# Transposing q, k and x by DMA instead of on TensorE in a fused attention and SwiGLU kernel

## The chip, the cores and the metric

One core of one Trainium2 chip runs the whole kernel. The metric is the device time of one execution in microseconds; the median of the runs stands for a kernel. The engines are named as the profile names them: PE (matrix products and transposes), DVE and ACT (element-wise work), POOL and SP (here they issue DMAs). PE writes its results to PSUM, from where DVE or ACT copies them to SBUF.

## The reference

The kernel computes causal attention in a window of 64 positions for 8 batches of 8 heads, and puts the result through a feed-forward block.

```python
B, H, S, D = q.shape                        # 8, 8, 576, 64
scores = scale * np.matmul(q, k.transpose(0, 1, 3, 2))
rel = pos[:, None] - pos[None, :]
mask = (rel >= 0) & (rel < 64)
attn = softmax(np.where(mask, scores, -1e9))
attn_out = np.matmul(attn, v)
x = attn_out.transpose(0, 2, 1, 3).reshape(B * S, H * D)     # 4608 x 512
g = x @ w_gate                                               # 512 x 1536
out = (g * sigmoid(g) * (x @ w_val)) @ w_out                 # 1536 x 512
```

Inputs and the output are float32; the kernel computes in bf16 with float32 sums.

## The kernel before

**Tiling.** The 4608 tokens are cut into 36 chunks of 128 (index n) and 9 groups of 512 (index c, four chunks each). The batches are 576 long, so four of the chunks (4, 13, 22 and 31) lie across two batches and are loaded in two parts. Attention works on chunks, the feed-forward block on groups. These are the steps; each is a method that records its operations, with what they read and write, in a graph. `emit` then gives every engine its operations in the order of recording, with semaphore waits where data or a buffer's earlier use requires them. A DMA belongs to the queue of the engine that issues it, which waits in order like any other.

- `load_qk(n)` (line 269) loads q and k of a chunk by POOL's queue, with the cast to bf16, into rings `qn` and `kn` of `NQ` = 4 buffers, 128 tokens x 512. A buffer is written again only after `T` of four chunks before has read it.
- `load_v(n)` (line 319) loads v into `va`, a ring of `NV` = 8, by POOL's queue, and then copies it by two DMAs of SP's queue (lines 332 and 336) into `vb`, which holds v shifted by 64 tokens.
- `T(n)` (line 349) transposes k and q on PE, eight 128 x 128 blocks into one PSUM bank (line 360). DVE copies k's transpose into `kT` (line 365). q's transpose goes into `qz`, a ring of `NZ` = 4: for every pair of heads it holds two operands of 128 rows, each with one head's 64 rows and 64 rows of zeros, so that a product over 128 rows gives one head's scores. ACT copies the even heads (line 366) and DVE the odd ones (line 368); the zeros are written once at the start.
- `Sx(n, half)` computes the scores of four heads (line 389), ACT their exponential into `pt` (line 401), and DVE multiplies by the mask (line 407).
- `AV(n, half)` multiplies by v (lines 419 and 420); a column of ones in v gives the sum, DVE takes its reciprocal (line 426) and writes the normalised half of a chunk's x to `xb`, a ring of four (line 429).
- `X(n)` (line 432) transposes x of a chunk on PE, four blocks (line 441), and DVE copies the result into `xT` (line 448; ACT at line 450 in the first group), a ring of `NX` = 3 groups.
- `F(c, f)` computes gate and value of 128 of the 1536 columns for one group (line 466, eight products of 512 columns), ACT a tanh (line 472) and DVE two products (lines 474 and 476) into `hT`. It reads `xT` of all four chunks of its group.
- `O(c, u)` computes the output of 128 tokens (line 489, twelve products); ACT copies it to `ost` (line 494), a ring of four, and SP's queue stores it (line 496).

**Order.** `build` writes the order out by hand. The first group's attention and feed-forward run with special steps. From line 601 on, a loop over c and u does one slot per chunk: it loads chunk n + 4 with n = 4c + u + 4, does three F of group c, both halves of AV of chunk n and of Sx of chunk n + 1, one O of group c - 1, X of chunk n and T of chunk n + 2. Below, slot n is the pass of this loop with that n, so slots 8 to 11 have c = 1 and slot 35 is the last with attention. The last x of a slot with u = 3 is needed by the next slot's first F. The slots of the last group (c = 8) have no attention left.

Of the kernel before, what the change touches and what calls it, by code (L numbers as in the profile page):

```python
# [10 lines left out]
NCH = T // 128  # L11
# [137 lines left out]

class _Kernel:  # L150
    NQ = 4
    NV = 8
    NZ = 4
    NP = 4
    NX = 3
    NH = 2
# [9 lines left out]
    def alloc(self):  # L166
        nc = self.nc

        def sb(name, n, dtype=BF):
            return nc.alloc_sbuf_tensor(name, [128, n], dtype)  # L170

        def ring(name, cnt, n, dtype=BF):
            return [sb("%s%d" % (name, i), n, dtype) for i in range(cnt)]

        self.ident = sb("ident", 128)
        self.mask = sb("mask", 4 * 64)
        self.Wg = sb("Wg", NK * DFF)[:, :].rearrange("p (c f) -> p c f", c=NK)
        self.Wv = sb("Wv", NK * DFF)[:, :].rearrange("p (c f) -> p c f", c=NK)
        self.Wo = sb("Wo", NF * DM)[:, :].rearrange("p (c m) -> p c m", c=NF)
        hd = lambda t: t[:, :].rearrange("p (h d) -> p h d", h=H)  # L180
        self.qn = [hd(t) for t in ring("qn", self.NQ, DM)]
        self.kn = [hd(t) for t in ring("kn", self.NQ, DM)]
        self.va = [hd(t) for t in ring("va", self.NV, H * 80)]
        self.vb = [hd(t) for t in ring("vb", self.NV, H * 80)]
        self.kT = sb("kT", 4 * (T + 64))[:, :].rearrange("p (c t) -> p c t", c=4)
        self.qza = sb("qz", self.NZ * 4 * 2 * 128)[:, :].rearrange("p (r c e t) -> p r c e t", r=self.NZ, c=4, e=2)
        self.qz = [self.qza[:, r] for r in range(self.NZ)]
        self.fq, self.fk = [t[:, :].rearrange("p (h j d) -> p h j d", h=H, j=4) for t in ring("f", 2, H * 256, F32)]
        self.cq, self.ck = [t[:, :].rearrange("p (j h d) -> p j h d", j=4, h=H) for t in ring("c", 2, H * 256)]
        self.nmask = sb("nmask", 4 * 64)  # L190
        self.pt = [t[:, :].rearrange("p (h x) -> p h x", h=H) for t in ring("pt", self.NP, H * 192)]
        self.rc = ring("rc", 4, 4, F32)
        self.xb = ring("xb", 4, DM)
        self.xT = [t[:, :].rearrange("p (c t) -> p c t", c=NK) for t in ring("xT", self.NX, NK * 512)]
        self.sig = ring("sig", self.NS, 512)
        self.uu = ring("uu", self.NS, 512)
        self.hT = [t[:, :].rearrange("p (f t) -> p f t", f=NF) for t in ring("hT", self.NH, NF * 512)]
        self.ost = ring("ost", self.NO, DM, F32)
        self.wup = sb("wup", 1, F32)
        self.ps = [nc.alloc_psum_tensor("ps%d" % i, [128, 512], F32) for i in range(8)]  # L200
        self.rot = {"f": ([0, 1, 2, 3], 0), "o": ([4], 0), "a": ([5, 6, 7], 0)}
        self.n_s = 0
# [18 lines left out]
    def init(self):  # L221
# [6 lines left out]
        zz = self.qza  # L228
        g.op("dve", lambda e: e.memset(zz[64:128, :, :, 0, :], 0.0), writes=[("qz", i, p, 0) for i in range(self.NZ) for p in range(4)])
        g.op("dve", lambda e: e.memset(zz[0:64, :, :, 1, :], 0.0), writes=[("qz", i, p, 1) for i in range(self.NZ) for p in range(4)])  # L230
# [4 lines left out]
    def init_pt(self):  # L235
        g = self.g
        for i in range(self.NP):
            p = self.pt[i]
            g.op("dve", lambda e, p=p: e.memset(p[:, :, 64:128], 0.0), writes=[("pt", i, 0), ("pt", i, 1)])

    def init_va(self, i0):
        g = self.g
        for i in range(i0, i0 + 4):
            va = self.va[i]
            g.op("dve", lambda e, va=va: e.memset(va[:, :, 64:80], 1.0), writes=[("va", i)])

# [22 lines left out]
    def load_qk(self, n):  # L269
        i = n % self.NQ  # L270
        for dst, src, nm in ((self.qn[i], self.q, "qn"), (self.kn[i], self.k, "kn")):
            parts = list(self.segs(128 * n, 128))
            for j, (r, b, s, L) in enumerate(parts):
                d = dst[r:r + L]
                a = src[b, :, s:s + L, :].rearrange("h p d -> p h d")
                ks = [(nm, i, j)] if len(parts) > 1 else [(nm, i, 0), (nm, i, 1)]
                self.g.op("pool", lambda e, d=d, a=a: e.dma_start(d, a), writes=ks, dma=True)  # L277

    def first_loads(self):
        for half in range(2):  # L280
# [35 lines left out]
            else:  # L316
                g.op("dve", lambda e, d=d, a=a: e.tensor_copy(d, a), reads=[bk], writes=zk)

    def load_v(self, n):
        g = self.g  # L320
        i = n % self.NV
        va = self.va[i]
        parts = list(self.segs(128 * n, 128))
        for j, (r, b, s, L) in enumerate(parts):
            d = va[r:r + L, :, 0:64]
            a = self.v[b, :, s:s + L, :].rearrange("h p d -> p h d")
            ks = [("va", i, j)] if len(parts) > 1 else [("va", i, 0), ("va", i, 1)]
            g.op("pool", lambda e, d=d, a=a: e.dma_start(d, a), writes=ks, dma=True)  # L328
        vb = self.vb[i]
        lo = [("va", i, 0), ("va", i)]  # L330
        hi = [("va", i, 0 if len(parts) == 1 else 1), ("va", i)]
        g.op("sp", lambda e: e.dma_start(vb[64:128], va[0:64]), reads=lo, writes=[("vb", i, 1)], dma=True)
        if n + 1 < NCH:
            i2 = (n + 1) % self.NV
            vb2 = self.vb[i2]
            g.op("sp", lambda e: e.dma_start(vb2[0:64], va[64:128]), reads=hi, writes=[("vb", i2, 0)], dma=True)
# [12 lines left out]
    def T(self, n):  # L349
        g = self.g  # L350
        iq, iz = n % self.NQ, n % self.NZ
        qn, kn, qz = self.qn[iq], self.kn[iq], self.qz[iz]
        bank, bk = self.bank("a")
        tb = bank[:, :].bitcast(BF).rearrange("p (w c t) -> p w c t", w=2, c=4)
        ident = self.ident

        def pe(e):
            for w, src in ((0, kn), (1, qn)):
                for c in range(4):
                    r = e.transpose(tb[:, w, c, :], src[:, 2 * c:2 * c + 2, :], ident[:, :])  # L360
            return r

        g.op("pe", pe, reads=["ident"] + [(x, iq, j) for x in ("qn", "kn") for j in range(2)], writes=[bk])
        kd = self.kT[:, :, 64 + 128 * n:64 + 128 * n + 128]
        g.op("dve", lambda e: e.tensor_copy(kd, tb[:, 0]), reads=[bk], writes=[("kT", n, p) for p in range(4)] + [(bk, "k")])  # L365
        g.op("act", lambda e: e.activation(qz[0:64, :, 0, :], tb[0:64, 1], ACTF.Copy),  # L366
             reads=[bk, (bk, "k")], writes=[("qz", iz, p, 0) for p in range(4)])
        g.op("dve", lambda e: e.tensor_copy(qz[64:128, :, 1, :], tb[64:128, 1]), reads=[bk], writes=[("qz", iz, p, 1) for p in range(4)])

    def Sx(self, n, half, bias=False):  # L370
        g = self.g
# [37 lines left out]
    def AV(self, n, half):  # L409
        g = self.g  # L410
        iv, ip, ix = n % self.NV, n % self.NP, n % 4
        va, vb, pt = self.va[iv], self.vb[iv], self.pt[ip]
# [19 lines left out]
    def X(self, n, eng="dve"):  # L432
# [16 lines left out]
        else:  # L449
            g.op("act", lambda e: e.activation(xo, tb, ACTF.Copy), reads=[bk], writes=[("xT", it, u)])  # L450

    def F(self, c, f):
        g = self.g
        it, ih = c % self.NX, c % self.NH
        xT, hT = self.xT[it], self.hT[ih]
        i = self.n_s % self.NS
# [6 lines left out]
        def mm(bank, W):  # L463
            def pe(e):
# [10 lines left out]
             reads=[("sig", i), gk], writes=[("uu", i)])  # L475
        g.op("dve", lambda e: e.scalar_tensor_tensor(hT[:, f, :], uu[:, :], 0.5, V[:, :], ALU.mult, ALU.mult),  # L476
             reads=[("uu", i), vk], writes=[("hT", ih, f)])
# [28 lines left out]
    def build(self):  # L506
        W = lambda a, b: (self.load_w("g", a, b), self.load_w("v", a, b))

        def load(n):
            if n < NCH:  # L510
                self.load_qk(n)
                self.load_v(n)

        self.first_loads()
        self.init()
# [31 lines left out]
        self.X(3, "act")  # L547
        self.banks("a", [5, 6, 7])
        self.init_va(4)
        load(4)  # L550
        load(5)
        self.load_wo(0, 6)
        self.load_wo(6, 12)
# [43 lines left out]
        self.O(0, 3)  # L597
        self.X(7)
        load(10)
        load(11)  # L600
        for c in range(1, NFC):
            for u in range(4):
                n = 4 * c + u + 4
                live = n < NCH
                load(n + 4)
                self.F(c, 3 * u)
                if live:
                    self.AV(n, 0)
                    if n + 1 < NCH:
                        self.Sx(n + 1, 0)  # L610
                self.F(c, 3 * u + 1)
                if live:
                    self.AV(n, 1)
                    if n + 1 < NCH:
                        self.Sx(n + 1, 1)
                if c > 1:
                    self.O(c - 1, u)
                if live and c > 1:
                    self.X(n)
                self.F(c, 3 * u + 2)  # L620
                if live and c == 1:
                    self.X(n)
                if n + 2 < NCH:
                    self.T(n + 2)
        self.banks("o", [0, 1, 2, 3])
        for u in range(4):
# [44 lines left out]
```

## Time and profile before

| | |
|---|---|
| median of 3 runs | 376.63 us |
| the profiled execution | 376.83 us |
| its span (first to last instruction) | 375.1 us |
| granted PE clock over the span | 1.00 |
| DMA packets, bytes | 126158, 35.61 MB |

In the profile a line such as `L466 PE MATMUL ps<-xT,Wg` names the line of the kernel, the engine, the operation, what is written and what is read; behind it stand shapes, the count, busy time and the mean of one, and the idle time of the engine just before, with what ended it. The chain is the work that ended last, followed back from the end; in its listing the columns are the start, the length and what ran. A window's row gives busy time and count for PE, PE's weight loads, DVE, ACT and POOL, then the granted clock, the DMA share (packet time over 16 engines, which can pass 1 where packets overlap) and GB/s. The rows of DMA issues end with the KB of one and the median time from issue to landing.

### The profile page before, as it was taken

What the parts mean: (1) busy time and instruction counts of PE and PEld (TensorE: products, weight loads), DVE (VectorE), ACT (ScalarE), POOL (GpSimd) and SP (SyncE); (2) the same over time, 40 slices, a digit from 0 to 9 for tenths busy, and PEclk for the clock granted to TensorE, in tenths of its full rate; (3) what the DMA queues carried; (4) which work ended last, traced back from release to release, by engine and by line L of the source; (5) the groups of instructions that cost most, each with busy time, mean ns of one, the idle gap of its engine ahead of it and who ended that gap; (6) DMA issues with size and microseconds to landing.
All of it is one profiled execution on the core that took longest, in us unless ns stands there. A gap on an engine that the chain in (4) does not pass through costs nothing.

```text
span 375.1 us, 6635 instructions
## 1 busy us (share of the span) xinstructions
PE 352.3 (94%) x2624; PEld 192.0 (51%) x2624; DVE 254.6 (68%) x550; ACT 152.3 (41%) x260; POOL 107.5 (29%) x136
## 2 busy tenths in 40 slices
PE   1589999999899999999999999999999999999986
PEld 1564555555455555555555555555555555444432
DVE  6668876688867777777777777777777777655520
ACT  2553535435444444444444444444444444233311
POOL 8985525434222222322222222422220000000000
PEclk9999999999999999999999999999999999999999
DMA  9999999979957777777888787877771000010012
GB/s 236 202 201 175 204 173 205 169 47 91 84 71 85 86 86 87 82 88 87 90 87 89 78 94 86 86 83 77 78 82 37 30 29 30 28 58 28 28 38 104
DMA packets 126158, 35.61 MB, mean 95 GB/s; under 512 B 108272, under 2 KB 121520, under 8 KB 126128
## 3 DMA queue, kind: packets, MB, share of 16 engines
q0 software_dynamic: 113152, 17.83, 64.3%
q1 hardware_dynamic: 11920, 16.31, 13.5%
q10 hardware_dynamic: 1056, 1.05, 0.9%
q8 instruction: 21, 0.34, 0.4%
q14 instruction: 9, 0.07, 0.1%
HBM read 37.75 MB, written 9.44 MB: 126 GB/s over the span
## 4 chain that ended last, share of the span: by engine, by line
PE 81%; DVE 13%; ACT 3%; DMA 2%; issue 1%
PE ps L466 41%; PE ps L489 25%; PE ps L389 5%; DVE hT L476 4%; DVE uu L474 4%; PE ps L360 3%; PE ps L441 2%; PE ps L420 2%; PE ps L419 2%; DVE xb L429 2%; DMA f<-in_q_dram 2%; ACT sig L472 1%; DVE pt L407 1%; ACT qz L366 1%; PE ps L302 1%
## 5 line engine op out<-in xcount | busy, mean ns | idle before, releaser
L474 DVE SCALAR_TENSOR_TENSOR uu<-sig,ps 128x512 bf16<-128x512 bf16 x108 | 74.1, 686 | 65.1 <-ACT sig L472 65.1
L466 PE MATMUL ps<-xT,Wg 128*128 128x512 bf16 x432 | 111.0, 380 | 2.4 <-DVE xT L448 1.7
L466 PE MATMUL ps<-xT,Wv 128*128 128x512 bf16 x432 | 110.9, 379 | 0.0
L489 PE MATMUL ps<-Wo,hT 128*128 128x512 bf16 x432 | 98.7, 380 | 2.1 <-DVE hT L476 2.1
L472 ACT ACTIVATE sig<-ps 128x512 bf16<-128x512 f32 x108 | 64.0, 592 | 43.4 <-PE ps L466 43.4
L277 POOL DMA_DIRECT2D qn<-in_q_dram x36 | 30.4, 847 | 164.2 <-PE ps L360 161.3
L476 DVE SCALAR_TENSOR_TENSOR hT<-uu,ps 128x512 bf16<-128x512 bf16 x108 | 74.2, 687 | 3.7
L466 PEld LDWEIGHTS ps<-xT,Wv 128*128 128x128 bf16 x432 | 42.2, 98 | 51.0
L489 PEld LDWEIGHTS ps<-Wo,hT 128*128 128x128 bf16 x432 | 40.9, 98 | 46.9 <-DVE hT L476 2.7
L401 ACT ACTIVATE pt<-ps 128x512 bf16<-128x512 f32 x72 | 42.9, 596 | 33.2 <-PE ps L389 30.5
L466 PEld LDWEIGHTS ps<-xT,Wg 128*128 128x128 bf16 x432 | 38.2, 98 | 32.6 <-DVE xT L448 2.0
L494 ACT ACTIVATE ost<-ps 128x512 f32<-128x512 f32 x36 | 21.5, 597 | 74.8 <-PE ps L489 74.8
L366 ACT ACTIVATE qz<-ps 64x512 bf16<-64x512 bf16 x32 | 18.9, 590 | 57.8 <-DVE kT L365 57.8
L328 POOL DMA_DIRECT2D va<-in_v_dram x40 | 34.7, 875 | 1.3 <-DVE wup L226 0.8
L389 PE MATMUL ps<-qz,kT 128*128 128x128 bf16 x288 | 30.8, 225 | 2.0 <-ACT qz L366 0.4
L429 DVE TENSOR_TENSOR xb<-ps,rc 128x256 bf16<-128x256 f32 x72 | 30.6, 425 | 2.5
L277 POOL DMA_DIRECT2D kn<-in_k_dram x36 | 30.7, 858 | 1.2 <-DMA Wv<-in_moe_w_val_dram 0.8
L448 DVE COPY xT<-ps 128x512 bf16<-128x512 bf16 x32 | 13.6, 423 | 24.1 <-PE ps L441 24.1
L407 DVE TENSOR_TENSOR pt<-pt,mask 128x512 bf16<-128x512 bf16 x64 | 26.6, 416 | 1.5 <-ACT pt L401 1.4
L419 PE MATMUL ps<-vb,pt 128*128 128x65 bf16 x288 | 26.9, 194 | 0.1
L420 PE MATMUL ps<-va,pt 128*128 128x65 bf16 x288 | 27.0, 194 | 0.0
L419 PEld LDWEIGHTS ps<-vb,pt 128*128 128x128 bf16 x288 | 22.6, 98 | 7.3 <-DVE xT L448 0.2
(44 smaller groups left out, 198.6 us busy)
## 6 DMA issues: line engine op xcount, KB each, us to landing
out_dram<-ost SPq DMA_DIRECT2D x36, 256.0 KB, 2.0
vb<-va SPq DMA_DIRECT2D x71, 80.0 KB, 2.1
va<-in_v_dram POOLq DMA_DIRECT2D x32, 128.0 KB, 4.5
qn<-in_q_dram POOLq DMA_DIRECT2D x28, 128.0 KB, 3.4
kn<-in_k_dram POOLq DMA_DIRECT2D x28, 128.0 KB, 4.4
Wo<-in_moe_w_out_dram POOLq DMA_DIRECT2D x2, 768.0 KB, 19.2
Wg<-in_moe_w_gate_dram POOLq DMA_DIRECT2D x5, 256.0 KB, 12.7
Wv<-in_moe_w_val_dram POOLq DMA_DIRECT2D x5, 256.0 KB, 13.3
```

Source lines behind the costliest of these rows:

```text
L277: self.g.op("pool", lambda e, d=d, a=a: e.dma_start(d, a), writes=ks, dma=True)
L328: g.op("pool", lambda e, d=d, a=a: e.dma_start(d, a), writes=ks, dma=True)
L389: r = e.matmul(sv[:, w, c], self.kT[:, pr, k0:k0 + 128], qz[:, pr, :, 64 * w:64 * w + 64], start=not bias, stop=True)
L401: g.op("act", lambda e: e.activation(po, si, ACTF.Exp, scale=SCALE), reads=[bk], writes=[pk])
L419: e.matmul(av[:, j, :], pt[:, h, 0:128], vb[:, h, 0:65], start=True, stop=False)
L420: r = e.matmul(av[:, j, :], pt[:, h, 64:192], va[:, h, 0:65], start=False, stop=True)
L429: g.op("dve", lambda e: e.tensor_tensor(xo, av[:, :, 0:64], rb, ALU.mult), reads=[bk, ("rc", ir)], writes=[("xb", ix, half)])
L466: r = e.matmul(bank[:, :], W[:, kk, f * 128:f * 128 + 128], xT[:, kk, :], start=(kk == 0), stop=(kk == NK - 1))
L472: g.op("act", lambda e: e.activation(sig[:, :], G[:, :], ACTF.Tanh, scale=0.5), reads=[gk], writes=[("sig", i)])
L474: g.op("dve", lambda e: e.scalar_tensor_tensor(uu[:, :], sig[:, :], 1.0, G[:, :], ALU.add, ALU.mult), reads=[("sig", i), gk], writes=[("uu ...
L476: g.op("dve", lambda e: e.scalar_tensor_tensor(hT[:, f, :], uu[:, :], 0.5, V[:, :], ALU.mult, ALU.mult), reads=[("uu", i), vk], writes=[(" ...
L489: r = e.matmul(OB[:, :], hT[:, f, 128 * u:128 * u + 128], self.Wo[:, f, :], start=(f == 0), stop=(f == NF - 1))
```

## The change

- For chunks n >= `ND` = 12, which are prepared in the slots from c = 1, u = 1 on, `T(n)` is replaced by `TD(n)`: two transposing DMAs of SP's queue, one of k from `kn` to `kT` and one of q from `qd` to `qz`.
- `qd` is a new ring of four. q is loaded into it by two DMAs of POOL's queue, even heads and odd heads, each into its 64 of 128 columns; the other columns are zeroed once (`init_qd`). The transpose of this is `qz` with its zeros.
- `TD(n + 3)` is recorded after the first part of slot n, where `T(n + 2)` stood at the end of slot n.
- In the slots with c > 1, `X(n)` is replaced by `XD(n)`: one transposing DMA of SP's queue from `xb` to `xT`. It is recorded ahead of O, where X stood behind it.
- The copies of v (`copy_v`) are taken out of the load: for the chunks loaded in and just ahead of the loop they are recorded in slot n for chunk n + 3, behind XD (or behind X where c = 1).
- The ring of v shrinks from 8 to 6.

```diff
-    NV = 8
+    NV = 6
+    ND = 12
...
+        self.qd = [t[:, :].rearrange("p (c e x) -> p c e x", c=4, e=2) for t in ring("qd", 4, 1024)]
...
+    def init_qd(self):
+        for i in range(4):
+            for e_ in range(2):
+                d = self.qd[i][:, :, e_, 64 - 64 * e_:128 - 64 * e_]
+                self.g.op("dve", lambda e, d=d: e.memset(d, 0.0), writes=[("qd", i, 0), ("qd", i, 1)])
...
-        for i in range(i0, i0 + 4):
+        for i in range(i0, min(i0 + 4, self.NV)):
...
-                d = dst[r:r + L]
                 a = src[b, :, s:s + L, :].rearrange("h p d -> p h d")
-                ks = [(nm, i, j)] if len(parts) > 1 else [(nm, i, 0), (nm, i, 1)]
-                self.g.op("pool", lambda e, d=d, a=a: e.dma_start(d, a), writes=ks, dma=True)
+                ds, nk = [dst[r:r + L]], nm
+                if nm == "qn" and n >= self.ND:
+                    qd = self.qd[i][r:r + L]
+                    ds, nk = [qd[:, :, 0, 0:64], qd[:, :, 1, 64:128]], "qd"
+                ks = [(nk, i, j)] if len(parts) > 1 else [(nk, i, 0), (nk, i, 1)]
+                for z, d in enumerate(ds):
+                    az = a if len(ds) == 1 else src[b, z::2, s:s + L, :].rearrange("h p d -> p h d")
+                    kz = ks if len(ds) == 1 else [k + (z,) for k in ks]
+                    self.g.op("pool", lambda e, d=d, a=az: e.dma_start(d, a), writes=kz, dma=True)
...
+    def TD(self, n):
+        g = self.g
+        iq, iz = n % self.NQ, n % self.NZ
+        kn, qd = self.kn[iq], self.qd[iq]
+        kd = self.kT[:, :, 64 + 128 * n:192 + 128 * n]
+        ka = kn.rearrange("p h d -> p (h d)")
+        g.op("sp", lambda e: e.dma_start_transpose(kd, ka), reads=[("kn", iq, 0), ("kn", iq, 1)],
+             writes=[("kT", n, p) for p in range(4)], dma=True)
+        qo = self.qz[iz].rearrange("p c e t -> p (c e) t")
+        qa = qd.rearrange("p c e x -> p (c e x)")
+        g.op("sp", lambda e: e.dma_start_transpose(qo, qa),
+             reads=[("qd", iq, j) for j in range(2)] + [("qd", iq, j, z) for j in range(2) for z in range(2)],
+             writes=[("qz", iz, p, e) for p in range(4) for e in range(2)], dma=True)
...
+    def XD(self, n):
+        ix, it, u = n % 4, (n // 4) % self.NX, n % 4
+        xb = self.xb[ix]
+        xo = self.xT[it][:, :, 128 * u:128 * u + 128]
+        self.g.op("sp", lambda e: e.dma_start_transpose(xo, xb[:, :]), reads=[("xb", ix, 0), ("xb", ix, 1)],
+                  writes=[("xT", it, u)], dma=True)
...
         load(10)
-        load(11)
+        load(11, False)
         for c in range(1, NFC):
             for u in range(4):
                 n = 4 * c + u + 4
                 live = n < NCH
-                load(n + 4)
+                load(n + 4, False)
                 self.F(c, 3 * u)
                 if live:
                     self.AV(n, 0)
                     if n + 1 < NCH:
                         self.Sx(n + 1, 0)
+                if n + 3 < NCH and n + 3 >= self.ND:
+                    self.TD(n + 3)
                 self.F(c, 3 * u + 1)
                 if live:
                     self.AV(n, 1)
                     if n + 1 < NCH:
                         self.Sx(n + 1, 1)
+                if live and c > 1:
+                    self.XD(n)
+                    if n + 3 < NCH:
+                        self.copy_v(n + 3)
                 if c > 1:
                     self.O(c - 1, u)
-                if live and c > 1:
-                    self.X(n)
                 self.F(c, 3 * u + 2)
                 if live and c == 1:
                     self.X(n)
+                    self.copy_v(n + 3)
-                if n + 2 < NCH:
+                if n + 2 < NCH and n + 2 < self.ND:
                     self.T(n + 2)
```

More of the change, by code (lines that the diff above doesn't have):

```diff
@@ L317, in first_T, with load_v @@
                 g.op("dve", lambda e, d=d, a=a: e.tensor_copy(d, a), reads=[bk], writes=zk)
-    def load_v(self, n):
+    def load_v(self, n, copy=True):
         g = self.g
@@ L328, in load_v, with copy_v @@
             g.op("pool", lambda e, d=d, a=a: e.dma_start(d, a), writes=ks, dma=True)
+        if copy:
+            self.copy_v(n)
+    def copy_v(self, n):
+        g = self.g
+        i = n % self.NV
+        va = self.va[i]
+        parts = list(self.segs(128 * n, 128))
         vb = self.vb[i]
@@ L368, in T @@
         g.op("dve", lambda e: e.tensor_copy(qz[64:128, :, 1, :], tb[64:128, 1]), reads=[bk], writes=[("qz", iz, p, 1) for p in range(4)])
+    def TD(self, n):
+        g = self.g
+        iq, iz = n % self.NQ, n % self.NZ
[9 more added lines that the diff above has]
+             writes=[("qz", iz, p, e) for p in range(4) for e in range(2)], dma=True)
     def Sx(self, n, half, bias=False):
@@ L507, in build, with load @@
         W = lambda a, b: (self.load_w("g", a, b), self.load_w("v", a, b))
-        def load(n):
+        def load(n, copy=True):
             if n < NCH:
                 self.load_qk(n)
-                self.load_v(n)
+                self.load_v(n, copy)
         self.first_loads()
@@ L549, in build @@
         self.init_va(4)
+        self.init_qd()
         load(4)
```

## The prediction

> **What bounds the kernel now.** I read the page first: busy times, and the shares of the chain that ended last.
>
> ```profile
> span 375.1 us, 6635 instructions
> PE 352.3 (94%) x2624; PEld 192.0 (51%) x2624; DVE 254.6 (68%) x550; ACT 152.3 (41%) x260; POOL 107.5 (29%) x136
> PE 81%; DVE 13%; ACT 3%; DMA 2%; issue 1%
> ```
>
> PE is busy for 94% and carries 81% of the chain. That is an average, so I next read the chain in order of time around 200 us, in the part where attention and the feed-forward products run together (windows, then the last two lines from a later stretch of the same chain).
>
> ```profile
> 200.17 2.59 PE ps L489 x12
> 202.76 0.22 PE ps L441 x4
> 202.98 1.73 PE ps L466 x8
> 204.71 0.45 PE ps L360 x8
> 205.16 1.73 PE ps L466 x8
> 207.41 1.73 PE ps L466 x8
> 209.81 1.29 PE ps L489 x6
> ```
>
> ```profile
> 332.34 2.59 PE ps L489 x12
> 340.11 2.59 PE ps L489 x12
> ```
>
> A slot (one pass of the loop of lines 601 to 624, called by its n) is 209.81 - 200.17 = 9.64 us long, and every piece in it is PE: three F of 1.73, one O of 2.59, X of 0.22, T of 0.45, and the rest AV and Sx. Without attention, in the last group, a slot is 340.11 - 332.34 = 7.77 = 3 x 1.73 + 2.59. PE waits for nobody here, so what leaves PE in these slots comes off the time one for one, as long as nothing else becomes late.
>
> **The change, part by part.**
>
> *Transposes leave PE.* T(n) goes for n = 12 to 35 (it stood in slots 10 to 33), and X(n) goes for n = 12 to 35 (slots 12 to 35): 24 of each. By the chain's rows that is 24 x (0.45 + 0.22) = 16.1 us of PE. No PE work is added. A full slot becomes 9.64 - 0.67 = 8.97 us.
>
> *Copies out of PSUM leave DVE and ACT.*
>
> ```profile
> L366 ACT ACTIVATE qz<-ps 64x512 bf16<-64x512 bf16 x32 | 18.9, 590 | 57.8 <-DVE kT L365 57.8
> L368 DVE COPY qz<-ps 64x512 bf16<-64x512 bf16 x32 | 13.7, 427 | 1.0
> L448 DVE COPY xT<-ps 128x512 bf16<-128x512 bf16 x32 | 13.6, 423 | 24.1 <-PE ps L441 24.1
> L365 DVE COPY kT<-ps 128x512 bf16<-128x512 bf16 x32 | 13.3, 417 | 0.0
> ```
>
> Per slot 0.43 + 0.42 + 0.42 = 1.27 us of DVE and 0.59 us of ACT. DVE is 68% busy and off the path in these slots, so this is worth nothing by itself; it only lets xb be ready earlier (below).
>
> *Zeroing qd.* Eight memsets of 128 x 256 elements are added to DVE and two of the eight small ones on va go.
>
> ```profile
> 24.71 0.59 DVE L245 MEMSET va<- 128x128 bf16 x4
> 27.58 0.69 DVE L474 SCALAR_TENSOR_TENSOR uu<-sig,ps 128x512 bf16<-128x512 bf16 x1 [2.29 <-ACT sig L472]
> L225 DVE MEMSET mask<- 128x256 bf16 x1 | 0.3, 272 | 0.0
> ```
>
> At the row of the same size they cost 8 x 0.272 = 2.2 us, less 2 x 0.15 = 0.3. They stand right behind the memsets at 24.71, where DVE then waits 2.29 us for the first sig. 1.9 fits into that: price 0. If that cover were gone, it would be up to 1.9 us, once.
>
> *POOL.* Each of the 24 chunks loads q by two DMAs instead of one; three of them (13, 22, 31) lie across a batch and take two more instead of one, so 27 issues are added. v's ring goes from 8 to 6, so the load of v(n+4) now waits for AV(n-2); behind it on POOL stand q and k of n+5, which the transpose needs only in slot n+2.
>
> ```profile
> POOL qn L277 <- PE ps L360: 161.3, 27, 8.1
> SPq L496 <- ACT ost L494: 249.0, 35, 9.3
> ```
>
> ```profile
> 203.42 0.34 SPq L496 DMA_DIRECT2D out_dram<-ost  x1
> 203.80 0.46 SPq L332 DMA_DIRECT2D vb<-va  x1
> 204.30 0.60 SPq L336 DMA_DIRECT2D vb<-va  x1
> 207.34 0.90 POOL L328 DMA_DIRECT2D va<-in_v_dram  x1
> ```
>
> At 0.9 us an issue POOL goes from three to four issues, 3.6 us of a slot of 8.97. It waits 161.3 us in 27 times today, up to 8.1 us a time, so this is hidden: 0.
>
> *SP.* Three transposes (k, q, x) join one output and two copies of v. At the rows above, 0.34 to 0.60 us an issue, they add 1.0 to 1.8 us a slot; SP's queue waits up to 9.3 us for ost. I take 1.5 and price it at 0. The order within a slot is: k and q of n+3, then x of n, then the copies of v, then the output. The wait that is added is x's, for xb. Behind it are the copies, for vb that is read three slots later, and the output, whose buffers form a ring of four. Nobody waits for either.
>
> *The DMA engines.* k and x are 128 KB each and the padded q 256 KB: 512 KB a slot, read from and written to SBUF.
>
> ```profile
> 52.00:68.40 16.40, 15.40 (x140) 9.12 (x140) 9.45 (x27) 8.00 (x14) 10.33 (x14) 1.00 1.90 194
> 108.64:200.00 91.36, 91.02 (x690) 49.67 (x688) 66.06 (x145) 38.77 (x67) 27.81 (x33) 1.00 0.80 86
> ```
>
> ```profile
> q0 software_dynamic: 113152, 17.83, 64.3%
> q1 hardware_dynamic: 11920, 16.31, 13.5%
> ```
>
> ```profile
> out_dram<-ost SPq DMA_DIRECT2D x36, 256.0 KB, 2.0
> vb<-va SPq DMA_DIRECT2D x71, 80.0 KB, 2.1
> va<-in_v_dram POOLq DMA_DIRECT2D x32, 128.0 KB, 4.5
> qn<-in_q_dram POOLq DMA_DIRECT2D x28, 128.0 KB, 3.4
> kn<-in_k_dram POOLq DMA_DIRECT2D x28, 128.0 KB, 4.4
> ```
>
> The last two columns of the windows are the DMA share and GB/s. The share of the steady part is 0.80, but it reaches 1.90 from 52 to 68 us: packets overlap, so 1 is no ceiling, and a slot of 8.97 us can hold 8.97 x 1.9 = 17.0 us of packet time against 9.64 x 0.80 = 7.7 today. What 512 KB add is not in the trace. From q0 a packet takes 0.643 x 375.1 x 16 / 113152 = 34 ns, from q1 0.135 x 375.1 x 16 / 11920 = 68 ns. If a transpose moves pieces of 256 bytes (one row of one block), 2048 pieces over 16 engines are 128 each, 4.4 to 8.7 us; 7.7 + 8.7 = 16.4, still under 17.0. The lower bound is by q1's bytes: 0.135 x 375.1 x 16 / 16.31 MB gives 50 us per MB on one engine, and 0.524 MB / 16 costs 1.6 us. I take 4.4, as the pieces are like q0's, and price it at 0.
>
> *The wait that replaces X.* x(n) goes to F(n // 4). For u = 0 to 2 there is over a slot of time. For u = 3 the next slot's first F needs it: six times (groups 3 to 8).
>
> ```profile
> 201.49 0.42 DVE L429 TENSOR_TENSOR xb<-ps,rc 128x256 bf16<-128x256 f32 x1
> 202.82 1.03 PE L466 MATMUL ps<-xT,Wg 128*128 128x512 bf16 x4
> 204.99 1.03 PE L466 MATMUL ps<-xT,Wg 128*128 128x512 bf16 x4
> 206.28 0.43 DVE L368 COPY qz<-ps 64x512 bf16<-64x512 bf16 x1
> 206.29 0.59 ACT L366 ACTIVATE qz<-ps 64x512 bf16<-64x512 bf16 x1 [1.81 <-DVE kT L365]
> 207.39 0.69 DVE L474 SCALAR_TENSOR_TENSOR uu<-sig,ps 128x512 bf16<-128x512 bf16 x1 [0.68 <-ACT sig L472]
> ```
>
> xb is complete at 201.91, and the next slot's first F starts at 204.99: 3.08 us, less X and T between them (0.67) is 2.41. But uu at 207.39 waits 0.68 us for a sig that stood behind ACT's qz copy (206.29), and DVE itself copied qz until 206.71. Without them the whole DVE chain up to xb moves about 0.7 us ahead. That leaves 3.1 us from xb to F for the transpose, from issue to landing. Its bounds are the quickest plain DMA (2.0, the output) and the slowest load of that size (4.5, v). I take q's 3.4, since the x transpose is 128 KB in small pieces and is issued while the loads released by AV(n, 1) are in flight. With 0.2 us for the two semaphores the stall is 3.4 + 0.2 - 3.1 = 0.5 us, six times: 3 us. The bounds give 0 and 6 x 1.6 = 9.6.
>
> **The sum.** The profiled execution took 376.8 us, its span 375.1 and 1.7 around it; the median of the runs is 376.6. Span: 375.1 - 16.1 + 3.0 = 362.0; with 1.7 it is 363.7; put against the median, 0.2 lower, **363.5 us**. Its own range, from the bounds of the stall and the memsets, is 360 to 372.
>
> **The rivals.**
>
> *Late x (about 376 us).* If x lands behind the loads and behind one more DMA of SP (3.4 + 2.0 = 5.4 us), each of the six group boundaries stalls 5.4 + 0.2 - 3.1 = 2.5 us, 15 us in all, and the gain is eaten: 376.6 - 16.1 + 15 = 375.5. For it: loads and x share the engines, and the second half of xb is the last thing the slot makes. Against it: plain DMAs on this queue land in 2.0 to 2.1 us at the median.
>
> *Transposes as a stream, block after block (slower, about 467 us).* 512 KB are 16 blocks of 128 x 128. If the blocks are not spread over the engines but done one after another, the slot is as long as 16 blocks. At the rate of the copy of v, 80 KB in 2.1 us, a block of 32 KB takes 0.84 us, 16 take 13.4 us, and 24 slots lose 24 x (13.4 - 9.64) = 90 us: 376.6 + 90 = 467. It decides from 9.64 / 16 = 0.60 us a block. q and k would be late for Sx, and x stands behind both on the same queue. For it: no transpose by DMA is in this trace, and PE's own cost for a block is only 0.056 us (0.22 / 4), so the change moves work to where it is far dearer. Against it: the share of 1.90 is a mean over 16 engines, so the transfers of that stretch are spread over all of them.
>
> The Trainium skill speaks for this rival on the page "VectorE: DVE Perf Modes", section "The three transpose paths": it has the DMA path for a 128 x 128 bf16 block at 1309 ns. By it, an estimate, 16 blocks in series take 20.9 us a slot. The page "DMA: Bandwidth & Descriptors", section "Latency and other measured facts", speaks against it: an effective 261 GB/s for transposes, by which 512 KB are an estimated 2.0 us. No trace shown here decides between them.
>
> *PE is not the bound any more.* With 1.27 us of DVE work gone DVE has 6.9 - 1.3 = 5.6 us a slot (66.06 us in 91.36 us is 6.97 a slot of 9.64), ACT less: neither can bound at 8.97. I give it no chance of its own.
>
> **How the numbers follow.** A measurement of this kernel can tell about 2% from no change, so 369.1 and 384.2 us are the bounds. Forecast, with a stall of at most 1.6 us a boundary: 0.55. Late x: 0.20, of which 0.17 within 2% and 0.03 above it, where x takes over 7 us to land. The stream: 0.25, of which perhaps a third is mild (a block a little over 0.60 us, under 400 us) and the rest far up. Faster by over 2%: the forecast without its upper end, 0.54; within 2%: 0.17 + 0.01 = 0.18; slower: 0.25 + 0.03 = 0.28. The range goes from 358 (no stall at all, and a little from the DVE-bound slots 10 and 11) to 400, leaving out the far end of the stream.
>
> **What would show it.** Right: the chain's slot at 8.97 us with no transposes on PE after slot 11; PE idle before L466 of about 0.5 us at six places, with a DMA as releaser; the transposes of x landing in 3 to 4 us; SP's queue still mostly waiting. Late x: those six gaps at 2 us and more. The stream: gaps before L389 in every slot with kT or qz as releaser, and transposes of q landing in 8 us or more. The forecast is wrong if slots are longer than 9.2 us away from the boundaries, or if the transposes' issue on SP takes over 2 us each.

## The result, and the profile after

The changed kernel takes 355.45 us (median of 4 runs, 355.06 to 355.73) against 376.61 us before: a ratio of 0.9438, 95% interval 0.942 to 0.9457. One of the four runs of the kernel before took 747.17 us, where the other three took 376.50 to 376.63, and is left out of the ratio. The gain is 21 us; the time is 8 us under the forecast of 363.5 and 2.5 us below the range. The direction and the place of the gain were as forecast; its size was not.

The first two lines of the changed kernel's page:

```profile
span 353.6 us, 6112 instructions
PE 328.6 (93%) x2298; PEld 173.1 (49%) x2336; DVE 227.1 (64%) x484; ACT 140.8 (40%) x236; POOL 123.9 (35%) x163
```

The span is 21.5 us shorter. PE's busy share hardly moved (93% against 94%), so the shares tell nothing here; the chain in order of time does. One slot of it (start, length, what ran):

```profile
110.99 2.54 PE ps L532 x11
113.53 3.45 PE ps L509 x16
117.45 1.73 PE ps L509 x8
119.69 2.54 PE ps L532 x11
```

L532 is O and L509 is F in the changed kernel (one of O's twelve products is missing from these records). The slot is 119.69 - 110.99 = 8.70 us. The forecast was 8.97: the transposes' 0.67 us off 9.64. So 0.27 us more have gone from every slot, and no step of the prediction had named them.

Where they were can be seen in the kernel before, in a row that the prediction left unread. PE's weight loads, and DVE's timeline beside them, at the second Sx of the slot quoted in the prediction:

```profile
209.41 0.23 PEld L389 LDWEIGHTS ps<-qz,kT 128*128 128x128 bf16 x4 [0.15 <-DVE xb L429]
```

```profile
208.93 0.42 DVE L429 TENSOR_TENSOR xb<-ps,rc 128x256 bf16<-128x256 f32 x1
```

And the rows of waits, first before, then after (what waited, for whom, us in total, times, longest):

```profile
PEld ps L389 <- DVE xb L429: 4.7, 28, 0.4
```

```profile
PEld ps L425 <- DVE xb L465: 1.1, 5, 0.4
```

Attention has three PSUM banks. The second Sx of a slot writes the bank of the first AV, and may start when DVE has read that bank for xb (208.93 + 0.42 = 209.35, Sx at 209.41). Before, this wait came 28 times; after, 5 times.

Next come the waits for x and the DMAs of the changed kernel: first the chain at one of the two group boundaries where it runs through a DMA, then the DMA rows (those of the transposes have no KB), the packets of SP's queue, and the window of the steady part (its last two columns are the DMA share and GB/s):

```profile
199.42 3.18 DMA xT<-xb
202.65 1.90 PE ps L509 x8
```

```profile
out_dram<-ost SPq DMA_DIRECT2D x36, 256.0 KB, 2.7
vb<-va SPq DMA_DIRECT2D x71, 80.0 KB, 3.1
...
kT<-kn SPq DMA_TRANSPOSE x24, 5.2
qz<-qd SPq DMA_TRANSPOSE x24, 5.1
xT<-xb SPq DMA_TRANSPOSE x24, 3.0
```

```profile
q1 hardware_dynamic: 63376, 28.90, 41.0%
```

```profile
110.00:190.00 80.00, 79.47 (x549) 40.90 (x557) 53.16 (x112) 33.06 (x56) 31.85 (x41) 1.00 1.41 152
```

x is issued at 199.42, F starts at 202.65. The two slots around this boundary take 207.26 - 189.43 = 17.83 us by the starts of O, 0.43 more than 2 x 8.70; the next boundary costs 0.40, and the other four under 0.1 each. The stalls are 1.0 us in all.

### The profile page after: what moved, and what is told of

Same layout as the page of the kernel before. It is cut to its first block, busy times and chain, and to the rows that moved or that the text cites. A ratio compares the mean times of both kernels' runs of the same rounds, so it can differ in the third digit from the quotient of the medians.

```text
span 353.6 us, 6112 instructions
## 1 busy us (share of the span) xinstructions
PE 328.6 (93%) x2298; PEld 173.1 (49%) x2336; DVE 227.1 (64%) x484; ACT 140.8 (40%) x236; POOL 123.9 (35%) x163
## 3 DMA queue, kind: packets, MB, share of 16 engines
q1 hardware_dynamic: 63376, 28.90, 41.0%
## 4 chain that ended last, share of the span: by engine, by line
PE 75%; DVE 16%; DMA 3%; ACT 3%; issue 1%
PE ps L509 41%; PE ps L532 25%; DVE hT L519 5%; DVE uu L517 4%; PE ps L425 4%; DVE xb L465 2%; DMA xT<-xb 2%; PE ps L456 2%; PE ps L455 2%; DMA f<-in_q_dram 2%; ACT sig L515 1%; DVE pt L443 1%; PE ps L316 1%; DVE xT L484 1%; PE ps L424 1%
## 5 line engine op out<-in xcount | busy, mean ns | idle before, releaser
L509 PE MATMUL ps<-xT,Wg 128*128 128x512 bf16 x423 | 109.1, 379 | 3.7 <-DVE xT L484 1.9
L509 PE MATMUL ps<-xT,Wv 128*128 128x512 bf16 x432 | 110.9, 379 | 0.0
L532 PE MATMUL ps<-Wo,hT 128*128 128x512 bf16 x403 | 92.9, 379 | 3.8 <-DVE hT L519 1.3
L509 PEld LDWEIGHTS ps<-xT,Wv 128*128 128x128 bf16 x432 | 42.3, 98 | 51.0
L532 PEld LDWEIGHTS ps<-Wo,hT 128*128 128x128 bf16 x432 | 40.9, 98 | 46.9 <-DVE hT L519 2.7
L509 PEld LDWEIGHTS ps<-xT,Wg 128*128 128x128 bf16 x432 | 39.9, 98 | 45.0 <-DVE xT L484 2.3
L537 ACT ACTIVATE ost<-ps 128x512 f32<-128x512 f32 x36 | 21.5, 597 | 74.8 <-PE ps L532 74.8
L291 POOL DMA_DIRECT2D qd<-in_q_dram x54 | 39.0, 736 | 28.0 <-DMA qz<-qd 28.0
L456 PEld LDWEIGHTS ps<-va,pt 128*128 128x128 bf16 x288 | 20.2, 98 | 7.1
L425 PEld LDWEIGHTS ps<-qz,kT 128*128 128x128 bf16 x288 | 19.1, 99 | 2.6 <-DVE qz L390 1.1
```

Source lines behind the costliest of these rows:

```text
L291: self.g.op("pool", lambda e, d=d, a=az: e.dma_start(d, a), writes=kz, dma=True)
L425: r = e.matmul(sv[:, w, c], self.kT[:, pr, k0:k0 + 128], qz[:, pr, :, 64 * w:64 * w + 64], start=not bias, stop=True)
L456: r = e.matmul(av[:, j, :], pt[:, h, 64:192], va[:, h, 0:65], start=False, stop=True)
L509: r = e.matmul(bank[:, :], W[:, kk, f * 128:f * 128 + 128], xT[:, kk, :], start=(kk == 0), stop=(kk == NK - 1))
L532: r = e.matmul(OB[:, :], hT[:, f, 128 * u:128 * u + 128], self.Wo[:, f, :], start=(f == 0), stop=(f == NF - 1))
```

## The experiments

Two theories for the 0.27 us a slot. **A**: T's copies stood on DVE and ACT ahead of the first xb of a slot, so the bank came free late and the second Sx waited. **B**: transposes cost PE more than their own pieces in the chain, and DVE's copies are free, as the prediction had it. "Changed" below is the changed kernel. In runs 5 and 7 to 11 the letters are those of each expectation. Some of these runs differ from the kernel before by less than 2% in time; what tells A from B there is the length of the slot, which away from the group boundaries repeats within 0.01 us along a trace.

**1. The copies' time put back, without transposes on PE and without PSUM.** Added to the changed kernel at the end of slots 10 to 33:

```diff
+        g.op("dve", lambda e: e.memset(a[:, 0:440], 0.0), writes=[("fk", 0)])
+        g.op("act", lambda e: e.activation(z[0:64, :], a[0:64, 0:512], ACTF.Copy), reads=[("fk", 0)], ...)
+        g.op("dve", lambda e: e.memset(b[:, 0:440], 0.0), writes=[("fq", 0)])
```

> The changed kernel with three pieces of work added at the end of slots 10 to 33, where T stood: two DVE memsets of 128 x 440 float32 (about 0.42 us each) and one ACT copy of 64 x 512 that waits for the first of them. They touch SBUF alone; no PE work and no PSUM bank comes with them. Theory A (the part of the gain above T's and X's own PE time comes from DVE being late with xb, whose PSUM bank the second Sx of a slot needs): the slot grows from 8.70 to about 8.97 us and the second Sx waits for DVE's xb in every slot again; 24 x 0.27 = 6.5 us, about 362. Theory B (PE transposes cost PE more than their own pieces, DVE's copies are free): unchanged, 355.5 within 1 us.

377.88 us, ratio to the kernel before 1.0031 (1.0015 to 1.0046): the whole gain is gone. Waits, timeline and chain:

```profile
PEld ps L425 <- DVE xb L465: 17.2, 24, 1.2
PE ps L516 <- DMA xT<-xb: 5.3, 4, 2.0
```

```profile
121.94 0.42 DVE L465 TENSOR_TENSOR xb<-ps,rc 128x256 bf16<-128x256 f32 x1
...
122.42 0.40 PE L425 MATMUL ps<-qz,kT 128*128 128x128 bf16 x4 [0.71 <-DVE xb L465]
```

```profile
142.12 2.59 PE ps L539 x12
151.71 1.29 PE ps L539 x6
```

B falls: no PE work was added, and the slot is 151.71 - 142.12 = 9.59 us. A's wait is back, but at 0.71 us a slot, where A had expected about 0.27. The size is the lesson: before, PE with its transposes reached the second Sx only a little ahead of DVE, so the wait was short. Take the transposes' 0.67 us away from PE and leave T's copies, and PE just waits longer: the slot goes from 9.64 to 9.59 us and no further. The path over sig, uu, hT and xb, with these copies on it, was nearly as long as PE's own. The copies alone hold back 9.59 - 8.70 = 0.89 us a slot, 21 us in 24 slots. The rest of the 22 us are longer stalls for x, since xb comes later.

**2. The transposes put back on PE, without their copies.** In the changed kernel, eight blocks of kn and four of xb go through PE at the old places into the three banks; nobody reads them.

```diff
+                    self.only_pe([... ("kn", iq, 0), ("kn", iq, 1)], [kn[:, 2 * j:2 * j + 2, :] for j in range(4)] * 2)
+                    self.only_pe([... ("xb", ix, 0), ("xb", ix, 1)], [xb[:, 128 * j:128 * j + 128] for j in range(4)])
```

> The changed kernel with the PE transposes put back at their old places (eight blocks of kn at the end of slots 10 to 33, four blocks of xb after O in slots 12 to 35), into the same three PSUM banks, but nobody copies their results out or reads them. Theory A: only the PE pieces of 0.45 and 0.22 come back, slot 9.37 us, 16.1 us, about 371.5; the stalls for x's DMA at the six boundaries vanish, since F starts later, so it may be 370. Theory B: the whole gain goes, slot 9.64, 376 to 377.

370.07 us, ratio 0.9823 (0.9809 to 0.9838).

```profile
112.11 2.59 PE ps L543 x12
121.48 2.59 PE ps L543 x12
```

The slot is 9.37 = 8.70 + 0.67, as A has it: on PE the transposes cost their own pieces and nothing else.

**3. and 4. Each part alone.** q and k by DMA with x on PE, and x by DMA with q and k on PE:

```diff
 (3)
                 if live and c > 1:
-                    self.XD(n)
...
+                if live and c > 1:
+                    self.X(n)
 (4)
-    ND = 12
+    ND = 99
```

> One part alone: q and k by DMA, x on PE as before (X after O, DVE copy of xT). Theory A: T's 24 x 0.45 = 10.8 and the whole 6.5 for DVE and 0.6 in slots 10 and 11 are gained, no stalls for x: 376.6 - 17.9 = about 358.7. Theory B: two thirds of the blocks, two thirds of the gain: 376.6 - 15 = about 361.5.

359.52 us, ratio 0.9544 (0.953 to 0.9558): 17.1 us of the gain.

```profile
111.21 2.59 PE ps L532 x12
120.14 2.59 PE ps L532 x12
```

A slot of 8.93 = 8.70 + 0.22. T brings 0.45 + 0.27, X its 0.22 alone. The time is nearer to A's 358.7 than to B's 361.5.

> The other part alone: x by DMA, q and k on PE as before. Theory A: X's 24 x 0.22 = 5.4 us are gained and the wait for PSUM stays; xb is complete only 2.4 us ahead of the next F, so with a landing of about 3.0 us and 0.2 for the semaphores six boundaries stall about 0.8 us, 4.8 in all: about 376. Theory B: one third of the gain less small stalls, about 371.

371.56 us, ratio 0.9864 (0.9849 to 0.9879): 5.1 us, the time that B had named, but not by B's way.

```profile
122.45 2.59 PE ps L532 x12
131.87 2.59 PE ps L532 x12
```

```profile
PEld ps L425 <- DVE xb L465: 4.7, 28, 0.4
```

```profile
xT<-xb SPq DMA_TRANSPOSE x24, 2.3
```

The slot is 9.42 = 9.64 - 0.22, and the wait for the bank is what it was before, 4.7 us in 28 times. What A's number had wrong was the stall of 4.8 us: there is none to speak of. I had taken the distance from xb to F without T, which here still stands between them (3.08 - 0.22 = 2.86 us, not 2.41), and x lands in 2.3 us, not 3.0.

**5. x behind the output on SP's queue**, where X was recorded:

```diff
-                    self.XD(n)
...
                     self.O(c - 1, u)
+                if live and c > 1:
+                    self.XD(n)
```

> The changed kernel with x's transpose recorded where X stood, behind the copies of v and the output on SP's queue. Theory A (x has 3 us from xb to the next group's first F and just fits): the output waits for ost, so x is issued about 2.5 us later; at the six group boundaries F waits about 2.5 us more, 15 us, about 370; the slots in between stay at 8.70. Rival (x has slack, its place on the queue is free): 355.5.

384.61 us, ratio 1.0216 (1.0177 to 1.0255): 1.8 to 2.6% slower than before the change, from one step's place in a queue.

```profile
PE ps L509 <- DMA xT<-xb: 20.8, 6, 5.0
```

```profile
131.69 0.34 SPq L539 DMA_DIRECT2D out_dram<-ost  x1
132.08 1.28 SPq L492 DMA_TRANSPOSE xT<-xb  x1
```

O of this slot starts at 128.50, so x is issued 3.58 us behind it, where it was 112.28 - 110.99 = 1.29 in the changed kernel: 2.3 us later. x has no slack at the boundaries, as A says, but the price is twice the 15 us expected: waits of 20.8 us, and beside them PE's granted clock fell to a mean of 0.98 over the span (0.91 from 131 to 150 us, around the first of these waits, and 1.00 from 150 to 170). x also lands later here, in a median of 4.5 us and not 3.0; why wasn't tried by itself (more on this below the table of runs 8 to 11).

**6. The kernel before with T moved, all on PE.** This takes the 0.27 us without any DMA, if A holds:

```diff
+                if c > 1 and n + 2 < NCH:
+                    self.T(n + 2)
                 if c > 1:
                     self.O(c - 1, u)
...
-                if n + 2 < NCH:
+                if c == 1 and n + 2 < NCH:
                     self.T(n + 2)
```

> The kernel before, all transposes on PE, with one step moved: in the slots with c > 1 T(n + 2) stands ahead of O instead of at the end of the slot, so that its copies on DVE and ACT run beside O and no longer ahead of the first xb of the next slot. Theory A: the second Sx's wait for DVE's xb (0.17 to 0.27 us a slot) goes without any DMA, slot 9.40 instead of 9.64, about 5 to 6 us in 22 slots: about 371. Theory B (the 0.27 belongs to transposes on PE): 376.6, no change.

370.62 us, ratio 0.9846 (0.9832 to 0.9861).

```profile
PEld ps L389 <- DVE xb L429: 1.3, 6, 0.4
```

```profile
141.48 2.59 PE ps L489 x12
...
150.85 1.29 PE ps L489 x6
```

A slot is 150.85 - 141.48 = 9.37 us, and the waits fell from 28 to 6. So 5.8 of the 21 us (370.62 against 376.43 for the kernel before, measured beside it) lay in the order of the copies, and were to be had by moving one call. Which of T's three copies on DVE and ACT holds xb back was not tried one by one.

**7. k and q transposed twice**, the second time into tiles that nobody reads, to see how far the "stream" was:

```diff
                     self.TD(n + 3)
+                    self.TD2(n + 3)
```

> The changed kernel with the transposes of k and q issued twice, the second time into tiles that nobody reads: 1.75 times the transposed bytes. Theory A (neither SP's issue nor the DMA engines are near their limit): SP issues about 8.5 us in a slot of 8.70, the DMA share goes from 1.41 to about 1.75, slots stay under 9 us, and x comes somewhat later at the six boundaries: 357 to 367. Rival (the transposes are a stream that already nearly fills the slot): slots of 9.5 us and more, 375 and up.

376.86 us (ten runs, 373.68 to 379.62), ratio 0.9987 (0.9954 to 1.002): 21 us more than the changed kernel. One slot of SP's queue, without the two copies of v behind x:

```profile
116.96 1.24 SPq L398 DMA_TRANSPOSE kT<-kn  x1
118.30 1.24 SPq L402 DMA_TRANSPOSE qz<-qd  x1
119.60 1.26 SPq L493 DMA_TRANSPOSE c<-kn  x1
120.91 1.48 SPq L497 DMA_TRANSPOSE c<-qd  x1
122.48 1.27 SPq L505 DMA_TRANSPOSE xT<-xb  x1
...
125.12 0.54 SPq L552 DMA_DIRECT2D out_dram<-ost  x1
125.76 1.23 SPq L398 DMA_TRANSPOSE kT<-kn  x1
```

```profile
PE ps L522 <- DMA xT<-xb: 17.8, 5, 5.5
```

The queue issues without a gap: 125.76 - 116.96 = 8.80 us a slot, more than PE's 8.70. Away from the boundaries the slots are still 8.70 us, as A has it; the rival named the time, but not by its way, which was slots of 9.5 us. The time goes at the boundaries, where x is late twice over. At the first four it is issued 1.0 to 3.6 us behind its xb, which is the full queue, and then takes 4.6 to 6.1 us to land, where it took 2.8 to 3.2 in the changed kernel. The DMA share was 1.43 from 110 to 190 us and 1.52 from 190 to 270, where it had been 1.41 and 1.21; what makes the landing longer was not tried apart. The waits are 17.8 of the 21 us, and PE's granted clock was 0.94 from 110 to 190 us besides. With the transposes once, a slot takes 1.2 + 1.3 + 1.3 for them and 1.7 for the plain DMAs, 5.5 of 8.70 us.

**8. to 11. Going further.** 8: x by DMA from slot 8 and k and q from chunk 11 on, and x in two halves at the boundaries. 9: x by DMA in slots 8 to 10 as well, nothing else. 10: the transposes of k and q recorded behind x's. 11: 9 and 10 together.

```diff
 (8)
-    ND = 12
+    ND = 11
...
+                if live and u == 3:
+                    self.XD(n, 0)
...
-                if live and c > 1:
-                    self.XD(n)
+                if live:
+                    self.XD(n, 1 if u == 3 else None)
 (9)
-                if live and c > 1:
+                if live and (c > 1 or u < 3):
                     self.XD(n)
...
-                if live and c == 1:
+                if live and c == 1 and u == 3:
                     self.X(n)
 (10)
-                if n + 3 < NCH and n + 3 >= self.ND:
+                if c == 1 and n + 3 >= self.ND:
                     self.TD(n + 3)
...
                     self.XD(n)
+                    if c > 1 and n + 3 < NCH:
+                        self.TD(n + 3)
```

> A version that goes further: x by DMA from slot 8 on, k and q by DMA from chunk 11 on, and at the group boundaries (u = 3) x in two halves, the first issued as soon as the first half of xb is there. Theory A: the stalls at the boundaries (about 1.7 us) go, 4 x 0.22 + 0.45 us of PE go, and the slots with c = 1, where DVE sets the pace, lose 4 x 0.42 + 0.85 us of DVE: 350 to 353. Rival (the smaller transposes cost more on SP than they bring, or x is late in the slots with c = 1): 355 or more.

> The changed kernel with x by DMA in slots 8 to 10 as well (slot 11, a group boundary, keeps PE, as its slot is too short for SP). Theory A: 3 x 0.22 us of PE and 3 x 0.42 us of DVE go in slots where DVE sets the pace: about 354, 1 to 2 us under the changed kernel. Rival (SP's three transposes fill these short slots of 7.2 us and x is late there): no gain or up to 3 us more.

> The changed kernel with the transposes of k and q of chunk n + 3 recorded behind x's in the slots with c > 1. Theory A2 (x lands in 3.0 us and not in 2.3, as it does alone, because it shares SP's queue with the 256 KB of q issued just ahead): x lands in about 2.4, the stalls at the six boundaries (about 1.7 us) go: 353.8. Rival (the loads on POOL's queue, released by the same AV, hold it up): x still lands in 3 us, 355.5.

> Both of these edits together. Theory A: the gains add up, 352 to 353. Rival: as the two rivals say, 355 and more.

| | us | ratio to before, interval |
|---|---|---|
| changed | 355.45 | 0.9438 (0.942 to 0.9457) |
| 8 | 359.36 | 0.9544 (0.953 to 0.9558) |
| 9 | 354.85 | 0.9423 (0.9411 to 0.9435) |
| 10 | 359.34 | 0.9545 (0.9519 to 0.9571) |
| 11 | 355.29 | 0.9435 (0.9422 to 0.9449) |

None is told apart as better than the changed kernel; 9 is 0.6 us under it, within the intervals, and 8 and 10 are 4 us slower. 8 lost its 4 us at one place, in the short slots with c = 1, where SP's queue issued without a gap from 81.5 to 99.9 us. The halves of slot 11's x were ready at 91.09 and 93.29, were issued at 93.42 and 94.75, and the second took 5.0 us to land. The first F of group 2 waited 6.1 us for it:

```profile
93.42 2.53 SPq L497 DMA_TRANSPOSE xT<-xb  x2
```

```profile
PE ps L514 <- DMA xT<-xb: 7.2, 3, 6.1
```

In 10, x lands in a median of 3.4 us where 2.4 was expected, and PE waits longer for it (4.1 us in all, against 0.5): q's transpose ahead of it on the queue is not what makes it land late, so A2 falls.

The traces say more on what does. In the changed kernel the last of POOL's loads lands at 255.04 us, while k and q are still transposed in three slots and x in six. These are its DMA rows from 256 us on:

```profile
xT<-xb SPq DMA_TRANSPOSE x6, 2.3
kT<-kn SPq DMA_TRANSPOSE x3, 2.4
qz<-qd SPq DMA_TRANSPOSE x3, 2.7
```

Over the whole run the same rows have 3.0, 5.2 and 5.1. And in run 6, where nothing is transposed by DMA, the plain DMAs of SP's queue land late too:

```profile
out_dram<-ost SPq DMA_DIRECT2D x36, 256.0 KB, 4.0
vb<-va SPq DMA_DIRECT2D x71, 80.0 KB, 4.2
```

Before, they had 2.0 and 2.1. There a slot's loads had landed (v at 201.74) when the output was issued at 203.42; in run 6 v's load is issued at 199.90 and the output at 200.97, with the loads in flight. So the late landings go with the loads of q, k and v in flight beside them, as the rival of 10 says, and not with the transposes as such. No run took away the loads alone, so this is read from the traces and not shown by an experiment.

## Why the prediction was wrong

**The step that failed** is "Copies out of PSUM leave DVE and ACT": it called 1.27 us of DVE and 0.59 us of ACT a slot "worth nothing by itself", because DVE was busy for 68% and "PE waits for nobody here". PE did wait, 0.15 us at every second Sx, for a bank that DVE freed. The prediction had the piece in hand: it saw uu at 207.39 wait 0.68 us for a sig that stood behind ACT's copy of qz, and moved the chain up to xb ahead for it, but let only x's DMA gain by that. That xb also frees the bank for the second Sx is what it left out. Runs 1 and 6 show that T's copies cost 0.27 us a slot beside PE's transposes, 5.9 us in the 22 slots 13 to 34 (run 6 gets 5.8 us back).

**The sum, term by term.** By the ends of O, the slots 13 to 34 are 0.94 us shorter each. Of that 0.67 is PE's transposes, as forecast (run 2 shows the same 0.67), 14.7 us in 22 slots; 0.27 is the bank's wait, forecast 0, 5.9 us. X in slots 34 and 35 gives 0.4, as forecast. Up to the end of O in slot 12 the gain is 1.5 us (106.34 against 104.83), where the forecast had 0.9 for T on PE in slots 10 and 11; T's copies on DVE and ACT have gone from these slots too, and how the other 0.6 comes about was not tried. The stalls for x were forecast at 3.0 and are 1.0. -14.7 - 5.9 - 0.4 - 1.5 + 1.0 = -21.5, and the span is 21.5 shorter.

The stall has three parts. The distance from xb to F was taken as 3.1 us; where nothing waits it is 115.09 - 112.24 = 2.85:

```profile
111.82 0.42 DVE L465 TENSOR_TENSOR xb<-ps,rc 128x256 bf16<-128x256 f32 x1
115.09 1.03 PE L509 MATMUL ps<-xT,Wg 128*128 128x512 bf16 x4
```

So the chain to xb moved 0.4 us ahead of PE and not 0.7. Against that, x landed in 2.3 to 3.2 us at the six boundaries and not in 3.4, and the two semaphores took under 0.1 us and not 0.2. The error in the distance and those in the other two partly cancel; that the term came out only 2 us off is luck.

**The range.** Its lower end of 358 held no gain from DVE in the slots with c > 1. With the wait's row read as a bound (4.7 us and 1.4 for qz among PE's weight loads) it would have been about 352.

**Prices at nothing.** The zeroing of qd: eight memsets of 0.165 us, 1.1 in all, half of the 2.2 forecast.

```profile
L247 DVE MEMSET qd<- 128x128 uint32 x8 | 1.1, 165 | 0.0
```

SP: forecast 0.34 to 0.60 us a transpose, measured 1.19 to 2.35 (the longest for q, with a median of 1.40):

```profile
112.28 1.20 SPq L492 DMA_TRANSPOSE xT<-xb  x1
...
117.25 1.91 SPq L402 DMA_TRANSPOSE qz<-qd  x1
```

It was still hidden, but with 3 us of room in a slot and not 6; runs 7 and 8 spent that room.

The DMA engines: the forecast had 2048 pieces of 256 bytes a slot at 34 ns. SP's queue carried 63376 - 11920 = 51456 packets more, 2144 a slot, at (0.410 x 353.6 - 0.135 x 375.1) x 16 / 51456 = 29 ns. That was right.

**The rivals.** Late x did not come, but run 5 shows it as near: x issued about 2.3 us later, and landing later too, turns the gain into a loss. The stream did not come either: its bound was 0.60 us a block, and run 7 issued and landed 28 blocks in each slot of 8.80 us, 0.31 us a block. Four blocks of x by themselves land in 2.3 us (run 4). The Trainium skill's 1309 ns for one block ("VectorE: DVE Perf Modes", section "The three transpose paths") is therefore no price that adds up block by block here. No run here times a single block.

## What to carry to other kernels

A wait of 0.15 us in a slot does not say that only 0.15 us hang on its path. It says that two paths are nearly equal, and that shortening only one of them gains little. Price work on a non-bounding engine by what is behind it in its order, here a PSUM bank, and not by the engine's busy share. And look for the cheap move first: moving T ahead of O brought 5.8 us with no new mechanism.

## What the runs showed of the hardware

- A DMA transpose of 128 x 512 takes SP a median of 1.19 us (x) or 1.25 us (k) to issue, against 0.54 to 0.59 for the plain DMAs beside it; one of 128 x 1024 takes 1.23 to 2.35, with a median of 1.40, not twice as long.
- Eight DMAs in a slot, five of them transposes, filled SP's queue at 8.8 us (run 7), while the DMA share stayed at 1.43 to 1.52, below the 1.90 that it reached with weights.
- With no load in flight a transpose of 128 x 512 landed in 2.3 to 2.4 us and one of 128 x 1024 in 2.7 (changed kernel, from 256 us on). While loads were running the medians over the run came to 3.0 for x and 5.1 to 5.2 for k and q. The plain DMAs land later beside loads as well: the output in 2.7 us instead of 2.0 in the changed kernel, and in 4.0 in run 6, which has no DMA transposes.
